# Attention folded into an expert layer: the join of transposed scores two steps later, the first fold 256 columns wide, and the second block of input weights as a transfer of its own

## The chip, the cores and the metric

The kernel runs on one core of one Trainium2 chip. The metric is device time in microseconds (us) of that core. The chip's engines are called by the profile's names: PE (TensorE, matmuls; PEld is its weight load), DVE (VectorE), ACT (ScalarE), POOL (GpSimd), SP (SyncE, here an issuer of transfers). Each run is classed as fast or slow by its time and its clock; all runs told of here are fast, with a granted PE clock of 0.997 to 1.000. Within that, the clock still shows: the kernel before took 724.60 to 725.14 us in the six runs at 0.997 or 0.998, and 722.29 to 723.54 in all others.

## The reference, cut to what matters

```python
# B, N, C = 4, 6080, 256; 24320 tokens, d_ff = 2048
qn = q / (np.linalg.norm(q, axis=1, keepdims=True) + 1e-06)
kn = k / (np.linalg.norm(k, axis=1, keepdims=True) + 1e-06)
s = kn.transpose(0, 2, 1) @ qn / tau          # 256 x 256 per batch
a = softmax(s)                                # over the last axis
x = (v @ a).reshape(B * N, C)
h = x @ w_in
r = np.maximum(h, 0.0)
out = (scale * (r * r) + b) @ w_out
```

The scores of a batch are only 256 x 256, so the kernel never forms `v @ a`. It folds `a` into the weights, `wa = a @ w_in`, once per batch, and computes `h = v @ wa`.

## The kernel before

The output loop runs over 48 groups of 512 tokens, each in 16 steps. A step issues two matmuls of `h` (512 columns), then some seven of the output product of the group before (128 columns), and after them the "side" work filed under that step: loads, the next batch's scores, and that batch's finish. In the traces each engine starts its instructions in the order in which the program issues them: the timeline of DVE in the prediction shows two that need no transpose start at 163.39 and 164.53, behind one that waited for it until 162.78.

```python
    # finish of a batch (b >= 1): split the scores into two fp16 parts,
    # transpose each by DMA, join the parts again in fp32
    def split(part):
        ...                                   # DVE: hi = s * rk; lo = s * rk - hi
        for ch in range(CH):
            po(nc.sync.dma_start_transpose(
                out=st[part + "T"][:, :, ts(ch, P)], in_=st[part][:, ch, :]))

    def join():
        st["t"] = sm_pool.tile([P, CH, C], FP32, tag="sm_s", name="t_sb")
        po(nc.vector.tensor_add(st["t"], st["hiT"], st["loT"]))
    ...
    # order: table, norms, reciprocal, table, split hi, split lo, join, exp, exp, sums, folds
FIN = (-12, 0, 3, 3, 5, 7, 13, 15, 17, 20)    # steps of the first ten; folds at 23, 26, ...
...
    # folds: w_in block (j) times the exponentials, scaled into wa by ACT (m = 0) or DVE (m = 1)
    if self.b == 0:
        folds = [fold_both(0, P), fold_both(P, P)]
        folds += [fold_one(2 * P, NW - 2 * P, m) for m in range(CH)]
...
load_w_in(0, NW)                              # NW = 512
load_v(0)
load_w_in(NW, Dff)                            # columns 512 to 2047 in one transfer
...
for f in fin[6:13]:                           # batch 0: exponentials to the first 512 columns
    f()
```

`t_sb` in the profile is the joined tile, `t_hi` and `t_lo` the transposed parts. In the output product (seven products of Strassen's kind per group), three evictions by DVE named `u`, which take results out of PSUM, the memory that PE writes to, stand between matmuls that reuse the same PSUM tiles. So PE waits when one of them is late.

## Time and profile before

722.93 us is the median of the three runs before (722.61 to 723.24). The span of the profiled execution is 721.1 us.

| what | value | how to read it |
|---|---|---|
| PE busy in 80 to 150, 200 to 330, 350 to 500, 520 to 700 us | 70.00, 129.99, 149.99, 180.00 | no gap worth naming: here the matmuls are the time |
| PE busy in 150 to 170 us | 18.30 of 20 | one gap, in the finish of the second batch |
| PE busy in 38 to 60 us | 20.82 of 22 | the start still has gaps |
| DVE busy in 60 to 80 us | 18.91 of 20 | DVE carries part of the path here |

A gap of an engine that is the bound is worth its full length if nothing later takes it back. So the table asks of each change: which PE gap does it close, and does the next wait stand far enough behind?

### The profile page before, as it was taken

To read this page: it belongs to the slowest core of one execution; us is meant where nothing else is said; L and a number is where in the kernel's file an instruction comes from. 1 tells how busy PE (TensorE), PEld (TensorE's weight loads), DVE (VectorE), ACT (ScalarE), POOL (GpSimd) and SP (SyncE) were. 2 spreads that over 40 slices of the span, in tenths; PEclk is the share of its full clock that TensorE was granted. 3 is DMA by queue.
4 is the path that set the end of the run, shared out by engine and by line. 5 is a ranking of instruction groups with operands and counts; after the bars stand their busy time and mean duration, and the time that the engine had idled before them with its cause. 6 is when DMAs were issued, how large, how long until landed. Compare 5 with 4: busy or idle time off the path is not lost.

```text
span 721.1 us, 17651 instructions
## 1 busy us (share of the span) xinstructions
PE 700.3 (97%) x7485; PEld 505.4 (70%) x7485; DVE 626.3 (87%) x880; ACT 544.6 (76%) x589; POOL 109.1 (15%) x188
## 2 busy tenths in 40 slices
PE   4799999999999999999999999999999999999998
PEld 3556777776677777777677777777668777777777
DVE  4779999988889999999788898999888888888886
ACT  4479877887777777788777777878877777777875
POOL 4522331201101222110210222110000000000000
PEclk9999999999999999999999999999999999999999
DMA  9999998637474989353864777953423333321202
GB/s 236 208 259 140 176 174 141 110 103 126 97 118 105 154 146 141 80 118 78 144 134 89 129 135 131 159 93 83 103 64 78 89 75 74 97 59 45 83 30 75
DMA packets 89519, 84.27 MB, mean 117 GB/s; under 512 B 59648, under 2 KB 64576, under 8 KB 89440
## 3 DMA queue, kind: packets, MB, share of 16 engines
q0 software_dynamic: 25792, 43.40, 37.2%
q1 hardware_dynamic: 63072, 38.43, 21.3%
q8 instruction: 59, 0.97, 0.6%
q10 hardware_dynamic: 576, 1.31, 0.5%
q14 instruction: 20, 0.16, 0.1%
HBM read 78.91 MB, written 24.90 MB: 144 GB/s over the span
## 4 chain that ended last, share of the span: by engine, by line
PE 90%; DMA 5%; DVE 1%; ACT 1%; POOL 1%; issue 1%; DVEq 0%; ACTq 0%; POOLq 0%
PE h_ps L604 44%; PE o_ps L772 39%; PE s_ps L142 4%; PE wa_ps L309 2%; DMA qk<-in_q_dram 2%; DMA w_in<-in_moe_w_in_dram 1%; DMA qk<-in_k_dram 1%; ACT r L614 1%; DMA t_lo<-s_lo 1%; POOL qk L126 1%; PE o_ps L650 0%; PE o_ps L676 0%; ACT g L625 0%; DVE o_sb L632 0%; DVE S L698 0%
## 5 line engine op out<-in xcount | busy, mean ns | idle before, releaser
L614 ACT ACTIVATE r<-h_ps 128x1024 f16<-128x1024 f32 (+1 forms) x384 | 387.8, 1014 | 148.2 <-PE h_ps L604 146.3
L604 PE MATMUL h_ps<-vT,wa 128*128 128x512 f16 (+7 forms) x1632 | 451.9, 364 | 0.6 <-ACT r L614 0.4
L772 PEld LDWEIGHTS <-S 128*128 128x128 f16 x2944 | 197.9, 98 | 85.1 <-issue 0.4
L772 PEld LDWEIGHTS <-g 128*128 128x128 f16 x2208 | 155.0, 98 | 74.1
L627 DVE TENSOR_TENSOR g<-r 128x2048 f16<-128x2048 f16 (+2 forms) x150 | 174.5, 1164 | 16.9 <-ACT r L614 16.9
L772 PE MATMUL o_ps<-T,S 128*128 128x128 f16 x2208 | 183.2, 219 | 0.3 <-DVE S L698 0.2
L604 PEld LDWEIGHTS <-wa 128*128 128x128 f16 x1632 | 136.1, 98 | 23.0 <-issue 2.8
L772 PE MATMUL o_ps<-w_out,g 128*128 128x128 f16 x1472 | 134.2, 219 | 2.0 <-DVE u L632 2.0
L632 DVE SCALAR_TENSOR_TENSOR o_sb<-o_ps,s_out,u 128x256 f32<-128x256 f32 x138 | 66.3, 480 | 45.3 <-PE o_ps L772 42.2
L625 ACT ACTIVATE g<-r 128x1024 f16<-128x1024 f16 (+1 forms) x97 | 100.4, 1035 | 0.2
L142 PE MATMUL s_ps<-qk 128*128 128x256 f16 (+1 forms) x384 | 70.4, 284 | 13.7 <-ACT qk L133 8.9
L361 POOL DMA_DIRECT2D v<-in_v_dram x48 | 31.3, 656 | 266.1 <-DMA vT<-v 222.1
L632 DVE SCALAR_TENSOR_TENSOR u<-o_ps,s_out,rowconst 128x256 f32<-128x256 f32 x138 | 65.8, 476 | 0.0
L772 PE MATMUL o_ps<-w_out,S 128*128 128x128 f16 x736 | 63.5, 219 | 0.0
L772 PE MATMUL o_ps<-N,g 128*128 128x128 f16 x736 | 63.4, 219 | 0.0
L188 POOL DMA_DIRECT2D f<-f x30 | 26.3, 876 | 225.0 <-DVE f L178 199.3
L165 ACT ACTIVATE sq<-qk 128x1024 f16<-128x1024 f16 (+3 forms) x49 | 50.4, 1033 | 11.6 <-DMA qk<-in_k_dram 7.6
L700 DVE TENSOR_TENSOR S<-S,g 128x2048 f16<-128x2048 f16 (+1 forms) x47 | 56.4, 1200 | 1.2
L698 DVE TENSOR_TENSOR S<-g 128x2048 f16<-128x2048 f16 (+1 forms) x47 | 56.0, 1191 | 0.0
L704 DVE TENSOR_TENSOR S<-g,S 128x2048 f16<-128x2048 f16 x46 | 55.9, 1214 | 0.0
L702 DVE TENSOR_TENSOR S<-g 128x2048 f16<-128x2048 f16 x46 | 55.8, 1214 | 0.0
L142 PEld LDWEIGHTS <-qk 128*128 128x128 f16 (+1 forms) x384 | 33.1, 102 | 19.6 <-DVE qk L132 8.3
(75 smaller groups left out, 323.6 us busy)
## 6 DMA issues: line engine op xcount, KB each, us to landing
out_dram<-o_sb SPq DMA_DIRECT2D x46, 512.0 KB, 3.1
v<-in_v_dram POOLq DMA_DIRECT2D x47, 256.0 KB, 4.6
qk<-in_k_dram POOLq DMA_DIRECT2D x42, 256.0 KB, 5.9
qk<-in_q_dram POOLq DMA_DIRECT2D x42, 256.0 KB, 7.2
f<-f POOLq DMA_DIRECT2D x30, 128.0 KB, 3.1
vT<-v SPq DMA_TRANSPOSE x182, 3.2
w<-in_moe_w_out_dram POOLq DMA_DIRECT2D x4, 512.0 KB, 11.6
raw<-in_q_dram ACTq DMA_DIRECT2D x2, 512.0 KB, 6.7
```

Of the source, the lines that this page charges most:

```text
L142: po(nc.tensor.matmul(self.s_ps[:, ch, :], kc[:np_, j, ts(ch, P)], qc[:np_, j, :], start=(c == 0 and j == 0 and ch == 0), stop=(c == len(s ...
L165: po(nc.scalar.activation(out=st["sq"][:np_, 1, js, :], in_=kc[:np_, js, :], func=AF.Square))
L604: po(nc.tensor.matmul(dst, wa[:, ci, ts(m, P)], src, start=(ci == 0), stop=(ci == CH - 1), skip_group_check=True))
L614: po(nc.scalar.activation(out=r16[:, :, i % 2, :n], in_=h_tiles.pop((g, i))[:, :, :n], func=AF.Relu))
L625: po(nc.scalar.activation(out=dst, in_=src, func=AF.Square))
L627: po(nc.vector.tensor_mul(dst, src, src))
L632: po(nc.vector.scalar_tensor_tensor(out=dst, in0=src, scalar=s_out, op0=ALU.mult, in1=add, op1=ALU.add))
L698: po(nc.vector.tensor_add(T[1], A21, A22))
L700: po(nc.vector.tensor_sub(T[2], T[1], A11))
L702: po(nc.vector.tensor_sub(T[3], A11, A21))
L704: po(nc.vector.tensor_sub(T[4], A12, T[2]))
L772: po(nc.tensor.matmul(st[name][:, j, :], a()[:, i, ts(j, P)], w[:, i, :], start=first, stop=last, skip_group_check=True))
```

## The change

Its intent: give the transposes of the scores more time before DVE needs them, take the first fold in one piece of 256 columns in place of two of 128, and let the second block of `w_in` land without waiting for the third and fourth. The diff, whole but for context:

```diff
             if self.b == 0:
-                folds = [fold_both(0, P), fold_both(P, P)]
+                folds = [fold_both(0, 2 * P)]
                 folds += [fold_one(2 * P, NW - 2 * P, m) for m in range(CH)]
...
     load_w_in(0, NW)
     load_v(0)
-    load_w_in(NW, Dff)
+    load_w_in(NW, 2 * NW)
+    load_w_in(2 * NW, Dff)
...
-    for f in fin[6:13]:
+    for f in fin[6:12]:
         f()
...
-    FIN = (-12, 0, 3, 3, 5, 7, 13, 15, 17, 20)
+    FIN = (-12, 0, 3, 3, 5, 7, 15, 17, 19, 22)
...
-    for i, f in enumerate(fin[13:]):
+    for i, f in enumerate(fin[12:]):
         at_step(FOLDS[i], f)
```

## The prediction

> **What bounds the kernel now.** I read the page's first part, then the busy times by stretch, then what TensorE (PE) waits for, then the timeline around each wait. Page, part 1 (busy us, share of the span, instructions):
>
> ```profile
> PE 700.3 (97%) x7485; PEld 505.4 (70%) x7485; DVE 626.3 (87%) x880; ACT 544.6 (76%) x589; POOL 109.1 (15%) x188
> ```
>
> Busy share is not yet a bound, so I cut the span into stretches (columns: stretch, its length, PE, PEld, DVE, ACT, POOL busy, PE clock, DMA share, GB/s):
>
> ```profile
> 80.00:150.00 70.00, 70.00 (x761) 51.44 (x759) 66.58 (x98) 56.01 (x61) 18.58 (x28) 1.00 0.84 143
> 150.00:170.00 20.00, 18.30 (x205) 12.98 (x203) 17.64 (x27) 14.98 (x18) 2.29 (x5) 1.00 0.33 73
> ...
> 200.00:330.00 130.00, 129.99 (x1438) 95.29 (x1436) 118.59 (x167) 102.19 (x108) 21.27 (x33) 1.00 0.67 119
> ```
>
> PE is without a gap in the long stretches, at full clock. So its work sets the time there, and a change that neither removes nor adds matmuls can only win back its gaps: 1.70 us in 150 to 170, and those of the start. The waits of PE (total us, times, longest), the start's first loads left out:
>
> ```profile
> PE o_ps L772 <- DVE u L632: 2.0, 2, 1.7
> PE wa_ps L309 <- DMA w_in<-in_moe_w_in_dram: 0.4, 1, 0.4
> ...
> PE h_ps L604 <- ACT r L614: 0.4, 1, 0.4
> ```
>
> The first two are what the change aims at. VectorE (DVE) in the timeline around the first one:
>
> ```profile
> 160.49 0.48 DVE L632 SCALAR_TENSOR_TENSOR u<-o_ps,s_out,rowconst 128x256 f32<-128x256 f32 x1
> 162.78 0.69 DVE L266 TENSOR_TENSOR t_sb<-t_hi,t_lo 128x512 f32<-128x512 f16 x1 [1.81 <-DMA t_lo<-s_lo]
> 163.39 1.22 DVE L702 TENSOR_TENSOR S<-g 128x2048 f16<-128x2048 f16 x1
> 164.53 0.48 DVE L632 SCALAR_TENSOR_TENSOR u<-o_ps,s_out,rowconst 128x256 f32<-128x256 f32 x1
> ```
>
> and PE in the same time:
>
> ```profile
> 162.86 0.50 PE L772 MATMUL o_ps<-T,S 128*128 128x128 f16 x6
> 165.06 0.22 PE L772 MATMUL o_ps<-w_out,g 128*128 128x128 f16 x1 [1.70 <-DVE u L632]
> ```
>
> The join (t_sb, L266) stands at the head of DVE's in-order stream and waits 1.81 us for its last DMA transpose. Behind it wait a sum that needs no transpose (L702) and the eviction u at 164.53, and PE needs that eviction at 163.36. The tile view tells why only the second batch shows this:
>
> ```profile
> L261 SPq DMA_TRANSPOSE t_lo<-s_lo x6: 1189/1190/1193, 157.3 to 505.7; - x6
> DMA to landing us min/median/max: 2.3/2.3/4.0
> ```
>
> The transpose landed after 4.0 us there and after 2.3 elsewhere: third and fourth batch join at 335.42 and 508.08 without a wait.
>
> The start, timeline:
>
> ```profile
> 38.33 1.24 PE L309 MATMUL wa_ps<-w_in,eT 128*128 128x128 f16 x12
> 38.51 0.17 DVE L297 RECIPROCAL rs<-r_ps 128x2 f32<-128x2 f32 x1
> 38.77 0.99 ACT L302 ACTIVATE wa<-wa_ps,rs 128x128 f16<-128x128 f32 x3 [0.58 <-PE wa_ps L309]
> ...
> 39.41 0.59 PE L604 MATMUL h_ps<-vT,wa 128*128 128x512 f16 x2
> ...
> 40.42 0.39 PE L309 MATMUL wa_ps<-w_in,eT 128*128 128x512 f16 x1 [0.42 <-DMA w_in<-in_moe_w_in_dram]
> ```
>
> PE folds the first 512 columns of w_in, does one pair of real matmuls, then stands before the second block, because columns 512 to 2047 came as one transfer. The chain that ended last has that transfer in it (29.96 to 40.38, then this matmul), so the start is on the path.
>
> **What the Trainium skill says.** (1) "Perfetto Trace Analysis", DMA Optimizations: splitting transfers into smaller ones may let some work start sooner, where the DMA engines are generally idle. Here they are not idle (mean share 1.0 and more from 20 to 48 us), so a split makes no bytes faster; it only lets the first third be announced before the other two. (2) "DMA: Bandwidth & Descriptors", Issuing engines are not separate DMA queues: all issuers share the same 16 engines and their transfers interleave. The trace agrees: the slow t_lo is the one that still had completion packets out when the packets of the store issued at 159.91 had begun (from about 161.0). So a landing time is not a constant, and a consumer needs slack. (3) The same page's Rules for kernel authors: issue the DMA early, do compute, wait late. That is what moving the join does. (4) "TensorE: Matmul & The Clock Gate", Back-to-back issue gap: 134, 262 and 518 cycles at 2.4 GHz for 128, 256 and 512 columns, that is 56, 109 and 216 ns. The trace agrees for 512 (0.43 us per pair of h_ps in the chain) and for 128 (seven o_ps in 0.39 us).
>
> **The change, part by part.** The words of the title say "six half-slots" and "second batch"; the diff moves the join from 13 to 15, and the exponentials, sums and all later folds by two steps too, in batches two to four. I go by the diff.
>
> *Join two steps later.* No instruction is added or removed. A step is 0.43 us (two h_ps) + 0.39 (seven o_ps) = 0.82, so the join moves about 1.65 us down PE's program. By the loop, L702 (one step after the old place) and the eviction u of the second product (in the new step, ahead of the side work) now precede it. DVE from 160.97, where the first u is done: L702 1.2 us to 162.15, u 0.45 to 162.6; the join then finds t_lo at its old landing, 162.66, and waits 0.1 at most. The eviction is there by 162.65, ahead of 163.36: PE doesn't stop. What it wins, by the issue stream: from the group of six at 162.86 to the next matmul took 2.20 us; six at 56 ns are 0.34, so 1.86 lost. The next places that could take it back: the third u must be out before the fifth product's first matmul, some 2.6 us after 162.86, near 165.4. Join 0.65, square 1.2 and u 0.45 from 162.7 end at 165.0. It holds, with 0.4 to spare. In batches three and four the same six took 0.40 and 0.43 (337.29 to 337.69, 509.93 to 510.36), the eviction arriving just late: 0.06 and 0.09 come free as well. Sum: **2.0 us**.
>
> *Later folds on other steps.* Those on DVE (0.74 us each) go from steps 2, 8, 14, 4 of a group to 4, 10, 0, 6; those on ACT (0.68) from 15, 5, 11, 1 to 1, 7, 13, 3. I walked DVE through 186 to 195: with a fold at step 0 the first sum ends at 190.7 for a need at about 191.0; with one at step 6 the second u ends at 194.6 for 194.93. Narrow, not negative. **0**, at worst 0.3 a batch. The last fold ends ten steps before its use; it has room.
>
> *w_in's second block alone.* One more DMA issue on POOL (about 0.55 us, POOL is idle). In the trace's packet records the 256 packets of the 768 KB transfer start between 35.18 and 38.9 and the last ends at 40.33, 1.4 us after most. A third of them by bytes, 256 KB at the some 205 GB/s of that time, is 1.3 us: 35.2 to 36.5, with the same tail landed near 37.9. The rest (512 KB, 2.6 us) would land near 40.4, as before; it is first needed at step 3, at 42.59 now and about 41.9 then. So the wait goes and none takes its place.
>
> *First folded block 256 wide.* PE columns stay: eight matmuls of 128 and four of 256 are 8 x 56 + 4 x 109 = 884 ns, eight of 256 are 872. Evictions: ACT 128 wide 0.37 and 256 wide 0.48, DVE 0.35 and 0.48, so two fewer instructions and two fewer hand-overs of a PSUM buffer, off the path. But the first real matmul needs the wider block: folds from 38.33; ACT's half done near 39.25, DVE's (its two matmuls end near 38.93) near 39.46. The pair goes at 39.3 and 39.5 instead of 39.41 and 39.63, the second block's fold at 39.72 instead of 40.42. Both start parts together: **0.7 us**, by far the most of it from the load; the width alone would give nothing, as the wait for the load would swallow it. From 41 to 75 us ACT and DVE carry parts of the path, but their work starts from PE's, and so shifts with it.
>
> Sum: 722.93 - 2.0 - 0.7 = 720.2; for the narrow places I give back 0.2: **720.4 us**.
>
> **Rivals.** (a) *The stall returns elsewhere.* The transpose may land still later when the store's packets come at another moment, or the later join delays the third u. For it: only 0.4 us of slack, and a landing that varied from 2.3 to 4.0. Against: the two steps cover 1.65 us of the 1.81. It would leave 0.3 to 1 us of the stall: 721 to 721.5. (b) *The start's gain is absorbed.* ACT is busy 9.76 of the 10 us from 50 to 60, DVE 18.91 of 20 from 60 to 80. If the loads for w_out or batch two gated those, an earlier start would only lengthen waits there: about 721.1. Against: neither engine's list of waits names w_out, and PE's names no batch-two load. (c) *The moved folds cost PE:* up to 0.3 in each of three batches, 721.3. (d) *The stall was an accident of the profiled execution.* Then the timed runs never had it and win 0.7 and 0.15 only: 722.1. Against: the profiled execution took 722.91, the timed median is 722.93.
>
> **Range and chances.** All rivals leave gains between 0.8 and 2.9 us, and the runs of before spread 0.6. I take 719.6 to 721.8. 2% is 14.5 us; only a deadlock-like surprise gets there: faster 0.005, within 0.99, slower 0.005.
>
> **What would show it.** Right: PE's waits without the 1.7 us behind u and without w_in; PE busy 20.0 of 20 around the second join; the join of the second batch waiting under 0.3 us behind L702 and u; the second block's fold near 39.7; the span shorter by 0.7 us before 80 us and by 1.9 more at 170. Wrong: PE waits over 0.2 us for S or u where the folds now stand, a wait for w_in at step 3, or an unchanged time at 80 us.

## The result, and the profile after

The changed kernel takes 720.35 us (median of 4 runs, 720.19 to 720.56) against 722.87 us (4 runs, 722.61 to 723.24): 2.5 us less. The ratio is 0.9965, 95% interval 0.9948 to 0.9982. Ratios here and below are the mean time of one kernel's fast runs over that of the other's of the same rounds, so they are not quite the ratio of the medians quoted. A change under 2% is called "same", and so is this one; yet the difference is clear of noise, and it lies where the prediction put it.

The page of the changed kernel, part 1. Four PE matmuls fewer (the narrow folds), no other engine less busy to speak of:

```profile
PE 699.4 (97%) x7481; PEld 505.0 (70%) x7481; DVE 625.9 (87%) x879; ACT 544.5 (76%) x588; POOL 109.8 (15%) x189
```

Its stretches (length, busy time of PE, PEld, DVE, ACT, POOL, PE clock, DMA share, GB/s):

```profile
80.00:150.00 70.00, 70.00 (x758) 51.33 (x757) 66.59 (x96) 56.44 (x60) 18.56 (x28) 1.00 0.86 143
150.00:170.00 20.00, 20.00 (x223) 14.21 (x220) 18.36 (x29) 16.21 (x19) 3.17 (x6) 1.00 0.40 79
```

The gap of 1.70 us is gone from the second stretch. What PE still waits for (total us, times, longest; the first loads, and two waits of 0.2 us that stood there before too, left out):

```profile
PE h_ps L605 <- ACT r L615: 0.4, 1, 0.4
PE o_ps L773 <- DVE u L633: 0.3, 1, 0.3
```

The fold's wait for `w_in` is gone, and of the two waits for `u`, 2.0 us together, the long one. The remaining one, 0.3 us near 75 us, was there before. DVE around the second batch's join (start, duration, engine, line, instruction, and in brackets the idle time and what ended it):

```profile
159.83 0.48 DVE L633 SCALAR_TENSOR_TENSOR u<-o_ps,s_out,rowconst 128x256 f32<-128x256 f32 x1
160.22 1.22 DVE L703 TENSOR_TENSOR S<-g 128x2048 f16<-128x2048 f16 x1
161.36 0.48 DVE L633 SCALAR_TENSOR_TENSOR u<-o_ps,s_out,rowconst 128x256 f32<-128x256 f32 x1
162.29 0.69 DVE L266 TENSOR_TENSOR t_sb<-t_hi,t_lo 128x512 f32<-128x512 f16 x1 [0.46 <-DMA t_lo<-s_lo]
```

and PE:

```profile
162.20 0.50 PE L773 MATMUL o_ps<-T,S 128*128 128x128 f16 x6
162.53 0.22 PE L773 MATMUL o_ps<-w_out,g 128*128 128x128 f16 x1
```

The order on DVE has turned round: the sum and the second `u` first, the join after them. The join still waits, for 0.46 us, but nothing that PE needs at once stands behind it. PE goes from the six matmuls to the next in 0.33 us, where it took 2.20.

The tile's own view shows that the transposes did not become quicker; the slowest landed after 4.3 us:

```profile
L261 SPq DMA_TRANSPOSE t_lo<-s_lo x6: 1189/1191/1199, 156.6 to 503.1; - x6
DMA to landing us min/median/max: 2.3/2.3/4.3
```

The start:

```profile
38.34 1.03 PE L309 MATMUL wa_ps<-w_in,eT 128*128 128x256 f16 x8
38.52 0.17 DVE L297 RECIPROCAL rs<-r_ps 128x2 f32<-128x2 f32 x1
38.78 0.88 ACT L302 ACTIVATE wa<-wa_ps,rs 128x256 f16<-128x256 f32 x2 [0.59 <-PE wa_ps L309]
38.98 0.92 DVE L304 TENSOR_SCALAR wa<-wa_ps,rs 128x256 f16<-128x256 f32 x2 [0.29 <-PE wa_ps L309]
39.31 0.61 PE L605 MATMUL h_ps<-vT,wa 128*128 128x512 f16 x2
39.76 1.03 PE L309 MATMUL wa_ps<-w_in,eT 128*128 128x512 f16 x4
```

The last line is the fold of the second block. It starts at 39.76 without a wait, 0.66 us earlier than the 40.42 of before.

To see where the time leaves the kernel, one compares the issue times of the same output store in both timelines:

| store issued, before | same store, after | earlier by |
|---|---|---|
| 69.52 | 68.84 | 0.68 |
| 144.88 | 144.21 | 0.67 |
| 203.12 (past the second join) | 200.60 | 2.52 |
| 319.26 | 316.74 | 2.52 |
| 375.75 (past the third join) | 373.17 | 2.58 |
| 491.89 | 489.31 | 2.58 |
| 548.41 (past the fourth join) | 545.74 | 2.67 |
| 693.24 | 690.56 | 2.68 |

So 0.68 us come from the start, 1.85 from the second join, 0.06 and 0.10 from the third and fourth, and nothing moves anywhere else.

### The profile page after: what moved, and what is told of

Its sections match the earlier page's. It is cut to its first block, busy times and chain, and to the rows that moved or that the text cites. A ratio compares the mean times of both kernels' runs of the same rounds, so it can differ in the third digit from the quotient of the medians.

```text
span 718.5 us, 17642 instructions
## 1 busy us (share of the span) xinstructions
PE 699.4 (97%) x7481; PEld 505.0 (70%) x7481; DVE 625.9 (87%) x879; ACT 544.5 (76%) x588; POOL 109.8 (15%) x189
## 3 DMA queue, kind: packets, MB, share of 16 engines
q0 software_dynamic: 26064, 43.40, 37.7%
## 4 chain that ended last, share of the span: by engine, by line
PE 92%; DMA 4%; ACT 1%; DVE 1%; POOL 0%; issue 0%; ACTq 0%; POOLq 0%
PE h_ps L605 45%; PE o_ps L773 40%; PE s_ps L142 4%; PE wa_ps L309 2%; DMA qk<-in_q_dram 2%; DMA qk<-in_k_dram 1%; DMA w_in<-in_moe_w_in_dram 1%; ACT r L615 1%; PE o_ps L651 0%; POOL qk L126 0%; PE o_ps L677 0%; ACT g L626 0%; PE idle_ps L442 0%; DVE o_sb L633 0%; DVE sq L162 0%
```

## The experiments

Each run but the last three is the kernel before with the edit shown, timed in several rounds beside the kernel before on the same chip. All gave correct results.

### The join and what follows it, alone

```diff
-    FIN = (-12, 0, 3, 3, 5, 7, 13, 15, 17, 20)
+    FIN = (-12, 0, 3, 3, 5, 7, 15, 17, 19, 22)
```

> Only the join, exponentials, sums and later folds two steps later; the start as before. My theory (an early-standing join holds DVE's in-order stream): the 1.86 us behind the second join and the 0.06 and 0.10 at the third and fourth come back, nothing before 150 us moves; 720.9 us, PE busy 20.0 of 20 from 150 to 170. Rival (the two parts depend on each other, the stall went because the start moved the transposes against other transfers): the stall of about 1.7 us stays, 722.7.

Measured: 720.84 us (5 runs, 720.73 to 720.96) against 722.98 (11 runs, 722.29 to 724.96); ratio 0.9969, 0.9957 to 0.9981. PE is busy 20.00 of 20 us from 150 to 170. Before the second join the stores are 0.06 us later than before, after it 1.79 earlier, so the join alone brings 1.85 us. The join still waits 0.3 us for a transpose that landed after 4.1 us. The stall goes by the later join alone and not by anything in the start.

### The start, alone

```diff
-                folds = [fold_both(0, P), fold_both(P, P)]
+                folds = [fold_both(0, 2 * P)]
...
-    load_w_in(NW, Dff)
+    load_w_in(NW, 2 * NW)
+    load_w_in(2 * NW, Dff)
```

(with the two indices 13 turned to 12, as in the change)

> The wide first fold and the split load, the join as before. My theory: 0.68 us from the start on, the second join's stall stays near 1.7; 722.2 us. Rival (absorbed where ACT and DVE carry the path from 50 to 75 us): 722.8. Rival (the start alone cured the stall): 720.4.

Measured: 722.29 us (median of 6 runs) against 722.98; ratio 0.9983, 0.9971 to 0.9996. In the profiled execution the stores are 0.66 us earlier up to the second join; there the join waits 1.9 us in place of 1.81, and 0.55 of the gain is left. So the start's gain is not absorbed between 50 and 75 us. One thing was not expected: two of the six runs took 720.50 and 720.86, the others 722.24 to 723.00. The two are as fast as if the stall had not happened in them. They were not profiled, so that reading is argued and not shown; what makes the stall come and go is the subject of the runs below.

### The split load, alone

```diff
-    load_w_in(NW, Dff)
+    load_w_in(NW, 2 * NW)
+    load_w_in(2 * NW, Dff)
```

> Only the split load; the first folds stay 128 wide. My theory: the wait for the second block goes, PE reaches its fold at 39.84 instead of 40.42 us: 0.58 us, 722.3. Rival (the narrow first folds wait for buffers and hold PE as well): less than 0.3, 722.6 or more.

Measured: 722.64 us (722.39 to 722.95) against 722.98; ratio 0.9994, 0.9981 to 1.0007, which by itself decides nothing. The profile decides. The fold of the second block follows the first pair with no wait, at 39.83 us:

```profile
39.40 0.59 PE L605 MATMUL h_ps<-vT,wa 128*128 128x512 f16 x2
39.83 1.03 PE L309 MATMUL wa_ps<-w_in,eT 128*128 128x512 f16 x4
```

The stores are 0.60 us earlier up to the second join. There the transpose came so late that the join waited 2.0 us, and 0.37 was left to the end. The load gives the 0.6 us expected; the longer stall, which this edit does not touch, takes a part of it back.

### The wide fold, alone

```diff
-                folds = [fold_both(0, P), fold_both(P, P)]
+                folds = [fold_both(0, 2 * P)]
```

(again with the indices)

> Only the first folded block 256 wide; the load as before. My theory: PE arrives 0.1 us earlier before the same transfer and waits longer for it (0.5 to 0.7 us instead of 0.42); the fold still starts at 40.4: 722.9 us, the same as before within 0.1. Rival (the two fewer evictions free ACT and DVE for the stretch behind): 722.6 or less.

Measured: 723.31 us (722.94 to 724.50) against 722.98; ratio 1.0005, 0.9993 to 1.0017. The first pair of real matmuls starts at 39.37 in place of 39.41 and PE then stands before the same transfer:

```profile
39.37 0.61 PE L604 MATMUL h_ps<-vT,wa 128*128 128x512 f16 x2
40.44 0.81 PE L309 MATMUL wa_ps<-w_in,eT 128*128 128x512 f16 x3 [0.46 <-DMA w_in<-in_moe_w_in_dram]
```

The wait shown grew only to 0.46 us, less than expected, but the fold starts where it did, and the stores are earlier by 0.00. The width is worth nothing while the load is late. With the split load it is worth the difference between 0.60 and 0.66 to 0.68 us.

### The join one step later in place of two

```diff
-    FIN = (-12, 0, 3, 3, 5, 7, 13, 15, 17, 20)
+    FIN = (-12, 0, 3, 3, 5, 7, 14, 15, 17, 20)
```

> Only the join one step later (14 in place of 13); exponentials, sums and folds stay. My theory (what counts is which DVE work stands behind the waiting join): the sum L702 goes ahead of it, the eviction u still stands behind it. Join at 162.8, 0.65, u 0.45: PE goes on at about 163.9 instead of 165.06, so 1.1 to 1.2 us of the 1.86 come back and 0.7 stays; 721.7 us. Rival (any later join clears it): 720.9 to 721.0.

Measured: 721.91 us (721.37 to 722.31) against 723.12 (9 runs, 722.81 to 725.03); ratio 0.9977, 0.9964 to 0.9989: 1.2 us of the gain by the medians. DVE in the profiled execution:

```profile
160.91 1.22 DVE L702 TENSOR_TENSOR S<-g 128x2048 f16<-128x2048 f16 x1
162.47 0.69 DVE L266 TENSOR_TENSOR t_sb<-t_hi,t_lo 128x512 f32<-128x512 f16 x1 [0.35 <-DMA t_lo<-s_lo]
163.08 0.48 DVE L632 SCALAR_TENSOR_TENSOR u<-o_ps,s_out,rowconst 128x256 f32<-128x256 f32 x1
```

The sum has gone ahead of the join and hides most of its wait. The `u` that PE needs is still behind it. PE goes on at 163.61, against 165.06 before and 163.27 with the join two steps later. In this execution the transpose landed after 3.7 us and not 4.0, so its stall is a little milder than the median's. This is what an order effect looks like: one step brings a part, the second step brings the rest, although DVE does the same work in all three.

### The join two steps later, the folds where they were

```diff
-    FIN = (-12, 0, 3, 3, 5, 7, 13, 15, 17, 20)
+    FIN = (-12, 0, 3, 3, 5, 7, 15, 16, 17, 20)
```

> The join two steps later (15), first exponentials at 16, the second, the sums and all folds on their old steps. My theory (the moved folds cost nothing and give nothing): the same as the run with the whole FIN row moved, 720.9 us. Rival (the folds' new steps cost PE up to 0.3 in each batch): this one is faster than that by 0.3 to 0.9. Rival (they helped): slower by as much.

Measured: 720.90 us (720.69 to 721.46) against 723.12; ratio 0.9966, 0.9952 to 0.9980. The stores gain 1.85 us at the second join and 0.05 and 0.09 at the others, as with all of FIN moved (720.84, ratio 0.9969). The moved folds cost nothing and bring nothing.

### Why the transpose lands late: another moment for the instruction packets

The prediction laid the late landing at the door of the store that SP issues right behind the transposes. The packet records of the trace name another suspect. Here are the packets of the kernel before around the second t_lo transpose (queue, bytes per packet, count, first and last start, end of the last, all in us from the zero of the profile); queue 1 carries transposes and stores, the 4-byte packets are read as completions, as 32 of them follow the data of each transpose, and queue 8 is called "instruction" by the page:

```
queue 1    256 B x 256   159.82 .. 160.27   end 160.29   the transpose's data
queue 1      4 B x  14   160.47 .. 160.53   end 160.53   its completions
queue 8  16384 B x   1   160.53             end 161.54   an instruction packet
queue 1      4 B x  16   160.53 .. 160.62   end 160.63   completions
queue 1   4096 B x  58   160.93 .. 161.53   end 161.69   the store
queue 1      4 B x   2   161.53 .. 161.54   end 161.55   the last two completions
```

Thirty of 32 completions are out by 160.63. The last two start when the 16 KB packet ends. The trace's records of the semaphore on which the join waits show the same: fifteen of the transpose's sixteen updates came from 160.81 to 160.92, the sixteenth at 162.66. At the third and fourth join no such packet falls there, and all sixteen came together (335.19 to 335.29 and 507.85 to 507.96). At the fourth the 32 completions go out from 507.50 to 507.66, and the join starts at 508.08 without a wait. The page of before counts these packets (queue, kind: packets, MB, share of the 16 engines' span):

```profile
q8 instruction: 59, 0.97, 0.6%
```

0.97 MB over the 14,970 rows of PE's instruction stream (7485 matmuls and as many weight loads) is 65 bytes a row, so 59 packets are about one per 256 rows of PE. The Trainium skill, "Runtime: NRT & Kernel Launch", Instruction fetch mechanics, says the same: engines refill their instruction memory in blocks of 16 KiB, 256 instructions, over a DMA queue that the sequencer drives itself. If so, extra PE instructions at the start must move every later packet to an earlier place in the program. So:

```diff
     for c in range(NCH0):
         ...
+        if 3 <= c <= 6:
+            tiny_ps = h_tile("tiny_ps")[:, 0, :8]
+            for _ in range(12):
+                po(nc.tensor.matmul(tiny_ps, g0.tiles[c][1][:, 0, :P], g0.tiles[c][0][:, 0, :8],
+                                    start=True, stop=True, skip_group_check=True))
```

> The kernel before with 48 tiny extra matmuls in the first phase, where PE waits for data anyway (96 more rows in PE's instruction stream, so the 16 KB packet of the instruction queue that started at 160.77 beside the second t_lo transpose's completion packets should come some 3.5 us earlier in the program). Theory F (that packet holds one DMA engine for 1.0 us and with it this engine's completion): the second batch's t_lo lands within 2.6 us, the join waits under 0.2 us, PE's gap is gone; 721.0 us. Theory S (the store right behind the transposes delays them): landing stays near 4.0, 722.9 us.

Measured: 725.15 us (724.30 to 725.37) against 723.12; ratio 1.0020, 1.0007 to 1.0033. It is slower, and not what either theory had said in time. Three of its five runs were at a clock of 0.997 or 0.998; the two at 1.000 took 724.30 and 725.15, against 722.81 to 723.50 for the kernel before at 0.999 or 1.000. The trace answers the question all the same. The packet came at 156.94 us in place of 160.53, although the program at that point ran 0.62 us late: 4.2 us earlier in the program, which fits 96 rows at 18 rows per 0.82 us step (4.4 us). In the second batch it now fell on the first t_hi transpose, whose last two completions again started when it ended, at 158.28. SP issued t_lo later for it (its two t_hi issues took 3.34 us in place of 2.53), the join waited 0.90 us, and of the stall in this batch about 0.9 us was won. The second t_lo itself landed 2.30 us after its issue, with the store still issued right behind it. But the packets of the other batches moved too. In the third one came at 331.95 and its join now waited 0.68. In the fourth one came at 507.91, in the middle of the second t_lo transpose's completions, where before there had been none; fifteen semaphore updates came by 508.32, the sixteenth at 510.20. DVE in the fourth batch of this run:

```profile
510.32 0.69 DVE L266 TENSOR_TENSOR t_sb<-t_hi,t_lo 128x512 f32<-128x512 f16 x1 [1.90 <-DMA t_lo<-s_lo]
```

The fourth batch has caught the second batch's stall: 1.86 us between the stores on its two sides. The stall goes where the packet goes. (The stores of the first batch were 0.62 us late as well. Whether the extra matmuls did that is not shown: in this execution the granted clock was 0.5 from 26.1 to 29.5 us, and four matmuls of 512 columns took 1.69 us there in place of 1.03.)

### Why the transpose lands late: the store out of the way

```diff
-            store(g, 2 if g == NG - 2 else 0)
+            if g in [f - 5 for f in first_group[1:]]:
+                at_step((g + 2) * FT + 8, lambda: store(g))
+            else:
+                store(g, 2 if g == NG - 2 else 0)
```

> The kernel before, with the one store per batch that follows the t_lo transposes issued six steps later, behind the v transposes. Theory S (the store's packets delay the last completion): t_lo lands within 2.6 us, PE's gap goes, 721.0 us. Theory F (the instruction packet alone holds that engine, until about 161.8): the join waits about 0.9 instead of 1.81, PE loses about 0.9 instead of 1.86; 721.9 us. Neither: 722.9.

Measured: 722.96 us (722.77 to 723.14) against 723.12; ratio 0.9991, 0.9979 to 1.0004. The stall is as it was:

```profile
162.68 0.69 DVE L266 TENSOR_TENSOR t_sb<-t_hi,t_lo 128x512 f32<-128x512 f16 x1 [1.79 <-DMA t_lo<-s_lo]
```

The store's packets are gone from behind the transpose (SP issued it at 165.87), v transposes stand there in their place, and the 16 KB packet runs from 160.46 to 161.50. The store is cleared. The expectation that the packet alone would cost only 0.9 us was wrong: the last completions start at 161.50, and the join only at 162.68, 1.18 us after. Where no packet stands in the way that distance is 0.43 us (completions to 335.37, join at 335.80, third batch of the run above). So the packet delays the completion twice: about 1.0 us until it may start and some 0.75 us until it is seen. The skill offers a reason for the second: "DMA: Bandwidth & Descriptors", Queues, rings and completion order, says that the semaphore increment is a strongly ordered write that lands only after every earlier write of that DMA engine, across its queues. An instruction packet on the same engine would be such a write. The numbers agree with it; no run here takes that ordering away, so it is not shown.

### The changed kernel again, and two tries to go below it

The first is the changed kernel unedited. The others take it and give casts of `w_out` from ACT to POOL, since ACT is busy 10.00 of the 10 us from 50 to 60:

```diff
-        else:
+        elif i == 1 or i == 3:               # second try: elif i == 1
             po(nc.scalar.copy(out=w_out16[:, ts(i, 4), :], in_=w_pieces[i]))
+        else:
+            po(nc.gpsimd.tensor_copy(out=w_out16[:, ts(i, 4), :], in_=w_pieces[i]))
```

> The changed kernel itself, timed beside the two below: 720.35 us within 0.2, so the sum of the join alone (720.84 against 722.98, 2.1 us) and the start alone (0.7 us) is the whole.

> The changed kernel with the third piece of w_out cast by GpSimd in place of ScalarE. Theory (ScalarE, 10.00 busy of 10 us from 50 to 60, holds PE there): PE's 0.4 us wait for the relu near 59 us goes and its 9.47 of 10 us in that stretch rises; up to 0.5 us faster, 719.9. Rival (VectorE, busy 18.9 of 20 from 60 to 80, sets that stretch anyway, or GpSimd's cast slows it): 720.3 or slower.

> As above with the third and the fourth piece. Theory: no more than the first of them, 719.9, as the fourth cast comes behind the relu that PE waits for. Rival (two casts on GpSimd slow VectorE or delay the loads that GpSimd issues): 720.5 or slower.

Measured, against 722.97 us (11 runs, 722.48 to 725.14): the changed kernel 720.75 (720.33 to 721.29), ratio 0.9961, 0.9947 to 0.9976; one cast moved 720.75 (720.15 to 721.51), ratio 0.9961, 0.9948 to 0.9975; two moved 720.48 (720.25 to 720.62), ratio 0.9957, 0.9943 to 0.9971. The changed kernel is 0.4 us above its first median, outside the 0.2 expected, with the kernel before at 722.97 beside it; the two measurements agree by their intervals. The 0.4 us are not in the kernel: the core's own span was 718.5 to 718.8 us in these five runs and 718.4 to 718.7 in the first four. In its profiled execution the start gave 0.57 us in place of 0.68, the joins the same as before. Neither cast helped clear of noise. ACT became less busy (9.37 and 9.04 of 10), PE's wait of 0.4 us for the relu stayed as it was, and so that wait is not made by these casts. There is no version here that clearly beats the changed kernel.

## Why the prediction was right or wrong

**The bound.** Right. PE's gaps were what there was to win, and the last stores came 2.68 us earlier, won in the gaps named.

**The join.** Right in mechanism and size. Foreseen were 1.86, 0.06 and 0.09 us; the stores show 1.85, 0.06 and 0.10, and the run with the join alone 1.85 at the second join. That a one-step move brings only part shows that the order on DVE is the cause and not the amount of its work.

**The join's remaining wait.** The step "the join then finds t_lo at its old landing, 162.66, and waits 0.1 at most" failed: it waited 0.46 us. The prediction took the landing as fixed and DVE as ready at 162.6. With the earlier start DVE was ready at 161.84, 0.76 us sooner, but t_lo landed at 162.17, only 0.49 sooner: the sixteenth update followed the end of the instruction packet by 1.18 us, as before (1.12), and that packet had come only 0.42 earlier (160.11 against 160.53). Why it moved less than the program stays open. Four matmuls fewer on PE would put it later in the program, but the run with the wide fold alone has the same four fewer, and its packet came at 160.50 with the program where it was. In the other runs with the join two steps later, the wait was 0.31, 0.16 and 0.35 us. PE did not notice, since what it needs now stands ahead of the join.

**The reason of the late landing.** The prediction read the packets of the store as what delayed the transpose. That was wrong. With the store out of the way the stall stayed (wait 1.79 us), and with the instruction packets moved it went to another batch (1.90 us in the fourth). The reading had rested on two things near each other in time. The step that used it, "a landing time is not a constant, and a consumer needs slack", held all the same.

**The moved folds.** Right: 0, as the run with the folds in their old places shows.

**The load and the fold.** 0.7 us foreseen, 0.66 at the fold and 0.68 at the stores measured. The packet times in the prediction stand 0.24 us later than the profile's zero, from which all other times count (40.33 for 40.09), so its landing near 37.9 means near 37.7; the last packet of the block alone ended at 37.60, and no wait for the rest took its place at step 3. The extra issue on POOL was read as 0.55 us; the `w_in` issues take 0.70 to 0.75, which cost nothing here. The division was right too: the load alone 0.60, the width alone 0.00.

**The sum.** The 0.2 us given back for narrow places was not needed in the profile: no new PE wait appeared. The medians differ by 2.5 and not by 2.7 us, so 720.4 was met in part by luck: a term that did not exist made up for the difference between the profiled span and the timed runs.

**The rivals.** Absorption of the start's gain is out (0.66 us in the run with the start alone, still whole at 145 us). The stall coming back elsewhere is out for the changed kernel. "An accident of the profiled execution" holds a grain: the stall was in every profiled execution with the old join, but its size moved with the packet, and two timed runs of the start alone were faster by about the stall.

## What to carry to other kernels

In an in-order stream, ask not only when an instruction's operand lands but what stands behind it: here, moving a consumer of a DMA behind the work that the bounding engine needed next won the whole stall of 1.85 us, though the operand came no sooner, and a move by one step won only a part. Ask also whether a large load can be cut where its first consumer ends: here the fold waited for all three blocks until one had a transfer of its own (0.60 us), and the wider fold was worth nothing while the load was what it waited for. When one of several equal places stalls and the others do not, look at the packets around it and test the suspect by moving it; the neighbour in time may be innocent.

## What the Trainium skill lacked or had wrong

- "Runtime: NRT & Kernel Launch", Instruction fetch mechanics, calls the cost of crossing a 16 KiB block mostly hidden. Hidden from the fetching engine, perhaps; here each block is one 16,384-byte packet that took 0.88 to 1.8 us in the kernel before (59 of them), and where it fell among a transpose's completions the landing went from 2.3 to 4.0 us and PE lost 1.86 us. Adding 96 PE rows moved the packet by 4.2 us and the stall from one batch to another.
- "DMA: Bandwidth & Descriptors" lists refills in a runtime-internal queue row, and has an engine drain a whole packet of one row before it turns to another, but does not say that an instruction packet can so delay a transfer's completion, nor by how much. With one, the last completions started when it ended and the consumer 1.18 us after that; without one, 0.43 us.
- "TensorE: Matmul & The Clock Gate", Back-to-back issue gap, gives about 81 and 131 ns per matmul for 128 and 512 columns as the sustained rate of weight loads and matmuls in pairs. Here such pairs run at 56 ns (seven in 0.39 us) and 216 ns (two in 0.43 us), which is what it calls the isolated gap.
